# Attention with a gated feed-forward on one core: the maxima's split moves to VectorE, the output projection's operands come in two stages, and the order is written anew

## The chip, the cores and the metric

The kernel runs on one core of a Trainium2 chip. The core has a matrix engine (TensorE, PE in the profile; PEld is its weight loads), VectorE (DVE), ScalarE (ACT), GpSimd (POOL), and SyncE (SP), which here issues every transfer between the chip's memory (DRAM) and the on-chip buffers (SBUF). PE writes into PSUM, which has eight banks of 128 x 512 float32. The metric is the device time of one execution in microseconds. Lower is better.

## The reference

`x` is 2048 tokens of 512 numbers. There are 32 heads of 16 numbers and 1792 hidden units.

```python
xn  = layernorm(x)
q, k, v = heads_of(xn @ wqkv)                    # 32 heads, 16 wide
p   = softmax(q @ k.T * 16 ** -0.5)              # 2048 x 2048 for each head, no mask
s   = join(p @ v) @ wo
g   = silu(((xn @ w_gate) * (xn @ w_up)) @ w_down)
out = x + s * g
```

## The kernel before

**Numbers.** Most products are made of two roundings of each operand, "high" (the number cast to fp32r) and "low" (what the cast left out): three matmuls, high x high, high x low, low x high. So every operand of a projection has to be split first: a cast and a subtraction, on POOL for weights (`split_raw`, L247 and L250), hidden values (`hidden`, L435) and attention outputs (`o_split`, L763 and L764).

**Units.** Attention is cut into 32 units: 8 groups of four heads times 4 chunks of 512 queries. For a unit, `score` (L918) multiplies queries and keys into a PSUM bank, and VectorE reduces each bank to a maximum for each query over 512 keys (L920). When 64 of those are there, `maxima` (L926 to L929) takes the maximum over the four key chunks, negated, and splits it; `rest` (L936) transposes it on VectorE, stores it to DRAM (`MD`) and loads it back as two more rows of the unit's queries. `expo` (L946) then multiplies keys by queries with these rows, so that ScalarE's exponential (L948) is already shifted by the maximum. `pv` (L957) multiplies the exponentials with the values; a column of ones beside the values gives the sum. `heads` transposes (L984), divides (L971, L972), transposes back (L976) and stores the unit's heads to DRAM (`OD`).

**Outputs.** Beside the units run 218 "outputs": the projections, the feed-forward's gate, up and down products, and at the end the output projection. An output is a list of matmuls of 64 rows each (L465), done twice: once on the lower 64 rows of PE's array and later on the upper 64. Matmuls on the two halves run at the same time, as do the scores and exponentials of a unit's even and odd heads. `pv` uses all rows.

**The order.** PE, ScalarE and VectorE work in an order that is written by hand into a string, `ORDER`. Its letters: `f` and `F` the next matmul of an output on the lower and upper half, `o` a new output, `s`/`S` a score and its reduce, `t`/`T` a product for exponentials and the exponential, `v`, `w`, `z` one, two or three turns of `pv` (four heads each), `m` the maxima, `r` the rest of them, `x`, `c`, `b` the three steps of `heads`, `d` and `e` the evacuation of an output by VectorE or ScalarE, `l` a glance of ScalarE at a finished lower half (L495), `h` a hidden split, `y` the gate's silu, `Q` and a digit a call of `prepare`. A digit behind `s`, `t` or `o` names the PSUM bank that it takes. Instructions of POOL and the transfers of SP are put in order by the language's own scheduler after the mark `|` in the string (before it, POOL follows the string too); each engine and queue then works strictly in its order. So an instruction that waits holds up everything behind it on its engine.

**The feed-forward's end.** When a chunk's feed-forward is done, `silu` computes the gate for four tiles of 128 tokens in `y`; for the first three chunks each tile goes to DRAM (`YD`, L443) and is fetched again for the end.

**The end.** `prepare(c)` calls `o_split`, which loads chunk c's heads in four quarters of 128 numbers from `OD` and splits each on POOL. The first quarter goes through the raw buffer `w1r`, the second through `w0r`, the third and fourth through `wdr`, and each of these has one copy. The fourth quarter of chunk c holds groups 6 and 7, so it follows unit 28 + c; chunk 3's has only group 6, and group 7 is added by `final`. `z_out` then multiplies chunk c with `wo`, `end` (L787, L788) multiplies with the gate and adds `x`, and the result is stored. Chunk 3 is opened before (`open_out`) and closed after the last unit.

Of the kernel before, what the change touches and what calls it, by code (L numbers as in the profile page):

```python
# [44 lines left out]
0fFfFs3S4lzes5T1o0S3fT2fT4fFs1FfT5fFs3Ft2Fs4Ft1FfS5fFt2FfS3t4FfFfFs5S1efT2t3S4lwt6S5t2T3o1S4fFfFfS6fT5fFs4Ft2Fs3FfT6fF
fS5fT2s4Fmt3FfFs6FfFs5S2let4T3zo0T4rfS6fT3s5Ft2FfFs4Ft6Fs3FfT5fFfS2t6Fs4FfFt5FfS3fT6fFfS2s4S5elws3T6t1T2s4Fo5FfFt6Fs3F
fFs4FfT1fT2fFs3Ft6FfS4fT1fFfS2fFfS3et6T4lwxs2T1t0Fs3Ft6Fs4Ft1Fo2FfS0fFs3T6fFt4FfFfS1fT6fS0t3T4fFfFfS1fS6s3S0elzcs1T4s6
Fo5T3fFt0FfS4t1Ft3Fs6FfFt0Fs4FfT1fFfS6fT3s0FfFfS4efT1s6T3wfS0s4S6lt2T1o3FfFfFt0Ft2FfS4fFt1FfS6t0FfFfS4fT2t1Fs6FfS0fFt2
T4webfS6o1S0lt2T4fFfFfS5t6Fs2FfT0fS4fFs5T6fFt2FfFs0FfT6s4FfFfFs5T2ls0S6zems4T2o5T3fS0fT6fFfS2t4FfFt3S0fFt6S2fT4fFt0S3f
Fs6Ft2FfFfS4t3Fls0Ft6Fwers4T2s0Ft3Fs6Ft1Ft2Fo4FfFs0FfT3s1FfT6s2FfFfT3fS0fT1fFfS6fS2efS3t0T1lzt5S6s2T0t1Fo3FfFfS5t6FfS0  # L50
fT2fFs1Fs5T6fFfT0fFfS2t6Fs1FfFfFs5S0let6T2vxt4S1t6Fs5Fs0T2wcs1T4t6S5t2Fo0FfFs4FfT1fFs5FfT6s2FfT4fS1fFfT6fS5t2T4fFfFs1S
6lwet2S5t4Fs1Fo3Ft6FfS2fT5fFs1S4fT6fFt2FfS5fT1s6FfFt2Fs4FfFfS5efT1s6T2lzbs4T0s5Ft1Fs6Ft2Ft0Fo4FfFfS5fT1s2FfT6fS0fFfT1f
S5t2FfFfS6t1T0fFs5S2lwes6T1s5Ft0T3o2FfFfS1fFfT6s5Ft0FfS3t1FfS6fFt5FfS0mt3FfFfFs6S1efS5t0T3lzrt4S6o0Fs1T3t5FfFs4Ft6FfFf
S1fT3fS5t4Fs6FfFfT3fS1fT5fFfFs6Fls4S3et5T1wt2S6s4Ft5Fo1T3fFfS2fT6fS5t4FfFfS3t2Fs6Ft5FfFs4Ft2FfFfS3fS6efT5s4T2lwxt0S3t5
T2s6Fo4FfFfS0fFt3Fs5FfT6s2FfFfT3s0FfT5fS6fT2fFs3Fs0FfS5es6S2lzcs3T1s0Ft5T6o2FfFs1FfT3s5FfFfT0s6Ft1FfT3fS5fFfS0t6FfS1fF
s5T3fFt6T0lwes1T3t6S5t0Fo4FfFs3FfT1fS6fT5fFfS0t3Ft1Fs6FfFfS5t3FfS0fFfFs6S1let3S5zbs0T2t3S6t1Fo5FfFfS2t0Fs3FfFt6Fs1FfT2
t0FfS3fFmfFt6FfT2dfT1s3T0vt6S4s3T2fS1fT0whlrs4Ft6Fs3Ft2Ft0Fs1Ft6Fs4Fo3FfT2fS0fT1fFfS4fT6fS2fT0fFfS1s4FfS6et2T0lzt5S1o4
Ft2S6fFt0Fs5Ft1FfFfS6fT2fS0fT5fFs1FfT2fS6t0FfFfFs1Flt5T2s6Fs0Fwdxt5S1t2T6s0Fo3FfFfS5fT1fFfS2fT0s6Ft5FfFs1Ft0S2fFhfFfT5
fS6s1T0lwect5S2t0Fs6Fo1T4fFfS5fT2s0FfFt6Fs4Ft5Fs2FfT0s6FfFfT4fS5fFfS2fS0s6T4lzdho5T4s2T0t6FfS3fFfFfS4fT2fS0t3T6fFfFs4F
# [1061 lines left out]
```

## Time and profile before

| | |
|---|---|
| three runs | 1736.26, 1739.68, 1740.42 us; median 1739.68 |
| the profiled execution | 1738.24 us, its span 1736.5 us |
| mean granted clock of TensorE | 0.994 |
| busy: PE, DVE, ACT, POOL | 1710.6, 1427.1, 1222.9, 594.1 us |
| transfers | 145.81 MB, mean 84 GB/s |

The span is the time from the first to the last instruction. Lines such as L936 are lines of the kernel before. A row of a group has the line, the engine, the operation, the tiles written and read, the shapes and the count, then the busy time, the mean duration in ns and the idle time of the engine ahead of it. A row of a timeline has its start, its length, the engine and line, and, in brackets, how long the engine had been idle and what released it. A row of a waits view has who waited for whom, the total, how many times, and the longest.

### The profile page before, as it was taken

How to read it: one execution, taken by the hardware profiler on the slowest of the kernel's cores; microseconds unless marked ns; L12 is line 12 of the kernel's file. 1: busy time of each engine (PE TensorE's matmuls, PEld its weight loads, DVE VectorE, ACT ScalarE, POOL GpSimd, SP SyncE). 2: the span in 40 equal slices, each digit the busy share in tenths (PEclk: the TensorE clock that was granted, in tenths of full speed). 3: DMA queues.
4: the chain of work that ended last, by engine and by line, in shares of the span. 5: the costliest groups of instructions: out<-in, count | busy, mean ns of one | idle time of the engine just before them, and what ended most of it. 6: DMA issues, size and time to landing. Idle time of an engine off the chain costs nothing.

```text
span 1736.5 us, 35407 instructions
## 1 busy us (share of the span) xinstructions
PE 1710.6 (99%) x13792; PEld 1088.4 (63%) x13792; DVE 1427.1 (82%) x2401; ACT 1222.9 (70%) x2503; POOL 594.1 (34%) x681
## 2 busy tenths in 40 slices
...
DMA packets 119795, 145.81 MB, mean 84 GB/s; under 512 B 12620, under 2 KB 74060, under 8 KB 116940
## 3 DMA queue, kind: packets, MB, share of 16 engines
...
## 4 chain that ended last, share of the span: by engine, by line
PE 93%; DMA 2%; POOL 2%; issue 1%; DVE 1%; ACT 0%; POOLq 0%; SPq 0%; DVEq 0%
PE b L465 36%; PE pv L957 26%; PE b L946 15%; PE b L918 15%; DMA w0r<-in_wu_dram 1%; PE v L354 1%; DMA wdr<-OD 1%; POOL w0l L250 0%; DVE mx L920 0%; ACT e L948 0%; PE p L354 0%; DMA hh<-in_x_dram 0%; POOL dl L643 0%; DMA ks<-in_x_dram 0%; DMA w0r<-OD 0%
## 5 line engine op out<-in xcount | busy, mean ns | idle before, releaser
L920 DVE TENSOR_REDUCE mx<-b 128x1 f32<-128x512 f32 x2048 | 1277.4, 682 | 211.2 <-PE b L918 115.3
L948 ACT ACTIVATE e<-b 128x512 f32<-128x512 f32 x2048 | 1088.0, 601 | 375.8 <-PE b L946 230.3
L918 PE MATMUL b<-ks,qs 48*128 48x512 f32 x2048 | 749.8, 413 | 4.3 <-DVE mx L920 4.2
L946 PE MATMUL b<-qs,ks 50*128 50x512 f32 x2048 | 709.5, 416 | 3.4 <-DVE mx L920 3.4
L957 PE MATMUL pv<-e,V 128*32 128x512 f32 x4096 | 489.5, 598 | 0.0
L918 PEld LDWEIGHTS b<-ks,qs 48*128 48x128 f32 x2048 | 356.6, 185 | 142.7 <-DVE mx L920 57.7
L946 PEld LDWEIGHTS b<-qs,ks 50*128 50x128 f32 x2048 | 338.2, 185 | 161.0 <-ACT e L948 47.8
L957 PEld LDWEIGHTS pv<-e,V 128*32 128x32 f32 x4096 | 108.6, 109 | 231.8 <-issue 223.4
L465 PE MATMUL b<-fh,w1h 64*128 64x512 f32 x504 | 200.6, 400 | 0.2 <-DVE mx L920 0.2
L465 PE MATMUL b<-fh,w1l 64*128 64x512 f32 x504 | 198.8, 396 | 0.0
L465 PE MATMUL b<-fl,w1h 64*128 64x512 f32 x504 | 198.8, 395 | 0.0
L465 PE MATMUL b<-fh,w0h 64*128 64x512 f32 x500 | 198.4, 399 | 0.2 <-DVE mx L920 0.2
L465 PE MATMUL b<-fh,w0l 64*128 64x512 f32 x500 | 196.8, 396 | 0.0
L465 PE MATMUL b<-fl,w0h 64*128 64x512 f32 x500 | 196.8, 394 | 0.0
L465 PE MATMUL b<-dh,hh 64*128 64x512 f32 x448 | 161.9, 397 | 0.0
L465 PE MATMUL b<-dh,hl 64*128 64x512 f32 x448 | 159.0, 396 | 0.0
L465 PE MATMUL b<-dl,hh 64*128 64x512 f32 x448 | 158.9, 393 | 0.0
L247 POOL CAST w1h<-w1r 128x512 fp32r<-128x512 f32 x60 | 36.6, 611 | 270.3 <-DMA w1r<-in_wg_dram 97.4
L247 POOL CAST w0h<-w0r 128x512 fp32r<-128x512 f32 x60 | 36.6, 610 | 211.3 <-DMA w0r<-in_wu_dram 107.3
L465 PEld LDWEIGHTS b<-fh,w1h 64*128 64x128 f32 x504 | 93.9, 187 | 11.3 <-issue 3.5
L465 PEld LDWEIGHTS b<-fh,w0h 64*128 64x128 f32 x500 | 92.8, 186 | 8.5 <-issue 2.7
L465 PEld LDWEIGHTS b<-fh,w0l 64*128 64x128 f32 x500 | 92.7, 186 | 8.4 <-issue 3.4
...
## 6 DMA issues: line engine op xcount, KB each, us to landing
...
```

Source lines behind the costliest of these rows:

```text
L247: cast = nc.gpsimd.tensor_copy(hi, raw)
L354: nc.tensor.matmul(o, l(d), r(d), start=k == d == 0, stop=k == 2 and d == ND - 1)
L465: nc.tensor.matmul(self.o, l[rows], r[rows], start=x == 0 and n == 0, stop=last and (x == 0 or self.engine is not None), skip_group_check= ...
L918: nc.tensor.matmul(o, QS[i][b:b + KB, pr, t * P:(t + 1) * P], k[b:b + KB, pr, kc * 512:(kc + 1) * 512], start=True, stop=True)
L920: nc.vector.tensor_reduce(MX[i][:, j, t, kc:kc + 1], o, axis=AX.X, op=OP.max)
L946: nc.tensor.matmul(o, k[b:b + KR, pr, kt * P:(kt + 1) * P], QS[i][b:b + KR, pr], start=True, stop=True)
L948: fst["recent"] = fst["exp"] = nc.scalar.activation(e, o, AF.Exp, scale=DH ** -0.5).ins.name
L957: nc.tensor.matmul(fst["pv"][32 * j:32 * j + 32], V[:, kt, h0:h0 + 32], es[j], start=kt == 0, stop=kt == NT - 1)
```

## The change

Four things change.

1. In `maxima`, the high part of the negated maximum is no longer a cast on POOL of VectorE's result. VectorE does the reduce a second time, with the rounded type as its output, and VectorE does the subtraction.
2. `prepare` takes 0 to 6. For chunks 0, 1 and 2 the first call prepares the first three quarters; 4, 5 and 6 prepare the fourth quarter of chunks 0, 1 and 2. Chunk 3 is prepared at once, as before.
3. `silu` no longer queues the store of a gated tile at once. It is kept back and queued when the fourth output after it begins.
4. `ORDER` is another string from shortly behind the mark `|` to the end. The numbers of each kind of work are the same. In the new string `Q0`, `Q4`, `Q1`, `Q5`, `Q3`, `Q2`, `Q6` follow each other; before they were `Q0`, `Q3`, `Q1`, `Q2`. `Q4` and `Q5` stand shortly behind the `b` of units 28 and 29, and `Q2` and `Q6` stand together behind that of unit 30.

```diff
-FfFfFfFfFfFs2FfFs5Flo3FfS1efS6fFfFfFfFs2FfFfFs5Fs1FfFfFfFo0S6lefS2fFfFfFs5FfFfFs1Fs6FfFfFfS2fFfF|o4S5lefS1fFfFs6FfFfFf
...
+FfFfFfFfFfFs2FfFs5Flo3FfS1efS6fFfFfFfFs2FfFfFs5Fs1FfFfFfFo0S6lefS2fFfFfFs5FfFfFs1Fs6FfFfFfS2fFfF|o4S5lefS1fFfFs6FfFfFs
...
         nc.gpsimd.tensor_tensor(y[:, t], e, y[:, t], op=OP.mult)
         if c < NC - 1:
-            dma(YD[c][:, t], y[:, t])
+            order_.kept_back.append([4, lambda: dma(YD[c][:, t], y[:, t])])
...
+            self.kept_back = []
...
         def low_product(self, k=None):
             if self.low is None:
                 self.low = next(self.outs)
+                for w in self.kept_back:
+                    w[0] -= 1
+                while self.kept_back and self.kept_back[0][0] <= 0:
+                    self.kept_back.pop(0)[1]()
                 self.low.open(pool(k))
...
-    def o_split(c, tiles):
-
-        for d, (oh, ol) in enumerate(tiles):
+    def o_split(c, ds):
+
+        for d in ds:
+            oh, ol = ops[c][d]
...
-        ops[c] = tiles
...
-    def prepare(c):
-        if c in (0, 3):
-            o_split(c, small_tiles())
+    def prepare(n):
+        if n > NC - 1:
+            o_split(n - NC, [ND - 1])
+            return
+        if n in (0, NC - 1):
+            ops[n] = small_tiles()
         else:
-            if c == 2:
+            if n == 2:
                 last_weights()
-            h, l = fst["big", c]
-            o_split(c, [(h[:, d], l[:, d]) for d in range(ND)])
+            h, l = fst["big", n]
+            ops[n] = [(h[:, d], l[:, d]) for d in range(ND)]
+        o_split(n, range(ND if n == NC - 1 else ND - 1))
...
         mm = keep.tile([P, 4, 2, 4], F32R, name="mm", bufs=2)
-        nc.gpsimd.tensor_copy(mm[:, :, 0], m)
-        nc.gpsimd.tensor_tensor(mm[:, :, 1], m, mm[:, :, 0], op=OP.subtract)
+        nc.vector.tensor_reduce(mm[:, :, 0], MX[i], axis=AX.X, op=OP.max, negate=True)
+        nc.vector.tensor_tensor(mm[:, :, 1], m, mm[:, :, 0], op=OP.subtract)
```

More of the change, by code (lines that the diff above doesn't have):

```diff
@@ L45 @@
[L45 to L59, printed above, removed]
@@ L160 @@
[L160 to L162 removed]
+FfFfFfFfFfFs2FfFs5Flo3FfS1efS6fFfFfFfFs2FfFfFs5Fs1FfFfFfFo0S6lefS2fFfFfFs5FfFfFs1Fs6FfFfFfS2fFfF|o4S5lefS1fFfFs6FfFfFs
+2FfFfS5fFmfFfFfFs1Flo3S6efFfFs2FfFfFfFfFfS5fFfFfFrfS1o0FlfFs6FefFs2FfFfFs5FfFfFfS1fFfS6fFfFo4S2lfFs5FefFfFfFs1FfFfFs6F
+fFfFfS2fS5fFo3FlfS1efFfT6s2Ft5T0fFfFfS1fS6t2Fs5FfFfT0fS1fFo2FlfT6s0FfT5fFs1FfFes6Ft0T5fFfFs1Ft4Fs6Ft0FfFfS5t1FfS4fFs6F
@@ new lines @@
+fS0et1T5lzs4T3s6Ft1Fo0FfT5s3FfT4fS1t6FfFfS5s3FfT4fFt6Fs1FfT5s4FfT3fS6fFt5S1lwet3S4s6T5t2Fo1FfFs3Ft4Fs5FfFt6S2fFfT3fS4f
+T5fS6fFt2S3fFfFfFs4S5let2S6zo3T0s4FfT2fS5t6FfFs0Ft4FfS2t5FfFfT6s0FfFfS4fT5fT2s6FfFs0Flt5T4wemrt2S6s0Ft5Fo4FfT1fS2t6FfF
+s0Fs5T1fFt2FfS6fFt1FfS0fT5fFfFfS6es2S1lt0S5wt3S6s2Ft0Fo1FfT5s3FfT6fFs2T0fFfT5fS3fT6fFs2T0fFt5Fs3FfFs6Fs2S0ewfT5o3S6lfT
+4fS2fT0s5FfFt6Fs4Ft2Ft0FfFfT6s5FfFs4FfT2fFfT0s5FfS6s4S2elwxt0Fs5Ft1Ft6Fo4S2fT0fFfS5fT1fS6fT2fFfS0t5Fs1Ft6FfFfFs0Fs2S5e
+fS1zlct6T3s0Ft2Fo5S1fFfT6fFfS0t3Ft1FfS2fFs6FfT0t3FfFfS2fT1fS6s0Fls3Fwes2T1t4T6s0Fo3FfFfS1fFfT2s0T4fFfS6t1FfT2fFt0S4fFs
@@ new lines @@
+6FfFfFs1Fls4T2t0Ft6Fwebt2S1t0Ft6Fs4Fo5FfT2fS1fFfT0fS4t6FfFt2S1fFt0FfS4fFmfS6es1S2zrfT0o4S6lfT3fS1fT2fFs0Ft6Ft3Fs1FfFt2
+Fs0Ft6FfFs1T3fT2fFfS0fFt6T1fT3wels0T2o6T1fS3fFt5Fs2FfFfT0s3FfT1fS5t2FfFs0Ft3Fs1Ft5S2fFfFfS0efS3s1S5lzs2T4s0Ft3Fo1FfT5f
+S4t2FfS3t0FfFs5Ft4FfT2s3FfFfS0fT4s5FfFfS3efS2t4T0lvxt6T4t0Fs5Ft3T2wct6S5t4S0t3Fo2FfFfS6fT5fS4fT0s3FfFfT6s5FfT4fFfFs3Ff
+Fs5S0les6T4zs3T1o5T4t0S6fFfFfS1fT3s4FfT6fFt0Fs1FfFt3S4t6FfFs0FfT1fT3s4Ft6FwebfS0o1S4lfT3fFt6FfS2t0FfFs4Ft3FfS6t2Fs0FfF
+t3S4fFfT6fFfFfS0es2T3lt4S6ws0T5s2Fo3T4fT6fFfS5fT0fS4mfFt2T6fFfS5s0Ft4FfFs2Ft6FfFfFs5Fls0S4et6Fzrt1S2s5Ft6Fo0T4fFfS1t2F
@@ new lines @@
+s6FfFfT5fS4fT1s2FfT6fT5fFs4FfFfT1wls2Fs4Fet6T5o1FfFfS3t2FfS6t4FfFfS5t3FfS2t6Fs4FfFfT3fFfFfS5es2T6ls4T3wxt0Fs5Ft6Fs2Ft3
+Fs4Fo0Ft5FfS6t2FfFfS3fT5fS4fT6fFfFfS3efS2fS5t6T4lwct1S3s2T6t4Fo5FfFs1FfT3fS6fT2fFs4FfT1s3Ft6FfFfS2t1Fs4FfFfS3efS6s2S1l
+zt0S4t3S6o2T1fFfFs0Ft4Fs3FfT6fFs1FfT0fT4s3FfFfS6fT0fT1fFt4Flbs3Ft0S6wet1S3t4Ft0Fo6S5fFfS1fT3fFfT4s5FfT0fT1s3FfFs4Ft5Fs
+0FfFs3T1fFt5S4zdhmrfT1o0S3lfT5fS4fT2fFs1Ft3Ft5Fs4Ft2FfFs1FfFfT3fS4t5FfS2fFt3FfS1t4S5lwet3S2s1Ft4Fo5T6fFs3Ft2FfFfS1s4T6
+fFfT3fS2fFfT6s1FfT4s3FfFfFs2S6lt4T1zdht4S3t1Fs2Fo6FfT0fS4fT3fS1fT2fS0fFfT4s3Ft1FfFfS2t4Fs0FfFs3Flt1Fs2T4vexs0T1s3Ft4Ft
@@ new lines @@
+5S2wct1S0s3T4t5Fo2FfFfS1fT0fS4fT3fS5fFt1FfS0fT4fFs3Ft1Fs5FfFs0T4lwdhs3T1s5T4t0Fo6FfFfS1fT3fS4t5FfFs0FfT1s3Ft4FfFs5Ft1T
+0fFfS4fS3fFs5T1lzebt0S4t1T2o3S5fFfFfS0fT4fS1fT5fFs2FfT0s4Ft1FfFs5Ft0Fs2FfFt1T4fFs5S0lwds2T1t4T5s0Fo6FfFfS1fFfT2s0Ft4Ff
+S5t1FfFfS2t0FfS4hmt5FfFs1FfS2fT0welrt5S4s1Ft0T3o2FfFfS5fT4s0FfT1fFs3Ft5Fs4Ft0FfS1fFfT5fFfS3s4FfS0s1T5lzdht5S3s4Ft0Fo1F
+fT6fS5t3FfT0fS4fFfT6fS5t3FfFt0S4fFs6FfT5s3FfFt0Flt4s6S5wexs3T0t4Fs6T2o5FfFs0Ft3FfFt4Fs6FfT2fS0fT3fFs4FfT6fS2fT0fS3fFfS
+4fFfS6s2S0lzcds3T4t6Fs2Fs0Ft1Fs4Ft3Ft6Fo2FfFt1FfS0fT3fT4fS6fFs1FfT0fT3fFfS6fT4fS1fFfFs0S3let6S4ws1T5t6Fs0Ft3Ft4Ft5Fs1F
@@ new lines @@
+t6Ft0Fwbs1T3o4T5s6FfFfT0fS3fT1fFfS6fT5fS0fT3fFs1Ft5FfS6fFfS0efT3s1S5lwmt2S6t3Fs0T1o5FfFs2FfT6s3FfT0fS1fFt2FfS6t3Ft0FfF
+s1T2rfFfFs6FfFfFfS1efS3fS0s6S2lzt4S1t3Ft0S6o2FfFfS4fT1s3Ft6FfFfS0fT4t1Fs3FfT6fFt4S0fFfFs3T1fFs6Fls0Ft4Fhs3T1zes6T4s0Ft
+1Ft5Ft3Fs4Fs6Ft1Fo0FfT5fT4fS3fFfS6fFt1Fs5FfT3fS4fT6vext1T3t6S5t2T4wcfS5fT1o3S6lfS2fT4fT5s1FfFt6Fs4FfFt5Fs2Ft6T1fFfFfS4
+fFfS2fFs5S6ls1Ft4Fzdhs2T4t5Fs6Fs1Ft0Ft4Fo2FfS5fT6fT0fFfS1t4FfT5s6FfFfT0fFbfS1fT4s6S5lwes1T0s6Ft4Fs5Ft3Ft0Ft1Fo4FfS6fFf
+S3fT5fS0fFfT1fS6fT5fFs3FfFs0S1lt5T6wds3T5t6T0s1Fo2FfFfS5fT3fFt6S1fS0mfFt5Ft3FfFfS1t6FhfS0t5FfFfFs1S3lwers0T6t5Fs1Ft4Ft
@@ new lines @@
+3Fs6Fo0FfS5fT1fFfS4fT6fT3fS5fFfS1t6Fs4FfFs5S3fFs1S6lzds4T5s3T1o6T2fFfFfS5fT4fFt1S3fFfT2fS5t4FfFs3T1fFt2Fhs5FfFt4Flt1Fw
+ext2T4s3Fs5T1o0FfFfS2fFt3Fs4FfT5t1FfFs2FfT3fS4fT5fFfS1fFt3Fls2S4zcdhs1T5s2T3o4T6fFfFs5FfFt1Fs2T3fFfS6fT5s1FfFt2Ft3FfS6
+fFfFfS1et5S2lt3S6wt0S1t5T3o2S6fFfFfS0fT1fS5fT6fFfT3s0FfFt1S5fT6fFs3Ft0FfS1fFfFs5Fls3Fs6Fs0T1zbdt1S5t3Fo6S0fT4fFs1Ft5Fs
+3Ft0Ft4FfFfS1fT5fS3fT0fFfS4fT1t5FfS3fFs0Ft1FfFfS4s3T5lzdmrs0T1t5Fs4T3o2FfFfS1fT0fT5fS4fFfT3fS1t0FfFs4T5fFt3FfS1t0FfFs4
+Ft5Fs3Fs1FfS0fFt4S5lzds3T4t1T0o5S6fFfFs4FfT3t1Fs6FfFfS0t4Ft3FfFt1S6fFs0T4fFfFfS3fT6t1FfS0fFfFs3T4lwdxs0T6s3T1s2T4vs0T6
@@ new lines @@
+t1Fs3Ft4Fs2Ft6Fs0Fo1FfFfT3fS4t2FfFfS0t6FfS3t4T2fFcfFs0FfFhs3S6fS4fS2zlds0T3t6S4t2Fo5FfFs3FfT0fFfS4fT6t2Fs3FfT0fFfS4fT6
+fS2fFs3Flt0Ft4Ft6Fs2Fwet0S3o4T6t1S2fFfFfS0fT3s6FfFt2FfS1s0T3fFfT6fT2fFfS1t3Fls0Fs6Fbzdhs1T2s0T3t6Fo5FfFs2FfT1s3FfFfT0f
+S6t2Fs1Ft3FfFfS0t6S2fFfT1fFmfS3t6S0lwert1S2t6T4o3S0fFfFs1Ft2FfS6t0FfFfS4fT1t2FfS6fT0fFs4FfT1fFs6S2ls0Fs4Fzdt1S6t2S0t4F
+o5FfFfS1fT6fFs0T2fFfT4s1FfFfT6s0T2hfFs4FfFt6Fs1Ft0T2wext6T0s4S1s2T3vfT6o4S1lfT0fS3fT2s6FfFt1S0fFt3Fs2FfFt1Fs6Ft0FfFs3F
+fFct1S2t6T0vds3S1t6T2vhs5S3s1T0t6T2vs5S0s3T6vt2S1fS5fT6fo0S3lfT2fT1fFfS6t5FfFs3Ft2Fs1Ft6FfS5fFs3T2fFt1T6fFfFs5S2fFt1S3
@@ new lines @@
+lzdbt6Fo5S2t1FfS3t4FfFfS6fT2s1Ft3FfFs4FfT2fS6t1T3fFfFfS4fFs2Fls6S1t3Ft4Fwdms2T3s6Fo4T1fFt0Fs3Ft2FfFfS6fT1fS0fT3fFfS2t1
+S6fFt0FfFrfS3s2T1lwds6T0t1Fs3Ft2Fs5Fo0FfT6fFfS3fT1fS2fT5s6FfFt1S3fFfT2fFs5FfFs6S1ls3T2zds5T2t6T1s3Fo4FfFfS2t5FfFfS3fT6
+fS1fT2fS5fFt6Fs3Ft1Ft2FfFt6S5fFs3T1lvyxt2S5t6Fs3S1wecs5T2s3Ft6Ft0Fs1Fo2FfT5fS6fT3fFfT0fS1fT5fS6fFfT3fS0t1Fls5Ft6Fs3Fwy
+dht1S0s5Ft6Ft3Fs4Fo1FfT0fFfS5fT6s3FfT4fS0fFt6T5fFfS3fFfFs0Fls4S6es5Ft3Fzbs0T2o4T3s6FfT5fFs2FfT0fS3fFt6Ft5Fs2FfFt0S3fFf
+T6fFt5T2dfS0fS3wylhs1T6s0Ft5Ft2Fs3Ft6Fo1FfFfS0fT5s2FfT3fFfS6t5Fs0FfT2fS3mfFfS6efS5t0S2lzyrt4Fs3S6t0Fo5T2fFt4FfFfS3t0Fs
@@ new lines @@
+6FfT2fFfS4fT3s0FfT6fFt2FfS4fFt3S0lwdhs4T6t2S0t3Fo1FfFs6FfS4fT2fT0fFfS3fT6fS2fT4fFs0Ft3Fs6FfFs2Fls4Ft3T0wexo6T3fS2fT0fS
+4fT5fS3fFfT2s0Ft4FfFs5Ft2Fs3FfFt4Fs0Ft2T5fFfFs3S4lzcdht2S0o5T3fS4fT1fFfS2fFfT0fS4t3Fs1Ft2FfFs0Ft4FfS3t1FfFfFs0Fls2S4et
+1T3ws0T6t1T3s2Fo4FfFs6FfT0s1FfT2fFs3Ft6S0fFfT1fFs2Ft6S3fFfT0fFfS1s2T6lzbdhs3T0o1Ft6S2t5FfFs0FfFfT3fS2t6Fs5Ft0FfS3fFt2S
+6fFfT5fFfFfS3et0T2ls6S5wms3T4t0Fs6Fo2T5fFfS4fT3s0FfT6s5FfFt4FfS3t0FfFrs6Ft4T5fFfS3fFfS0fS4fS6fT5zldt5S3t0Ft4S6o1FfFfS5
+fT3fFs6T0fFfT4fS5fFt3FfS6fT0s4FfFt3S5fFt6Fs0FfFfFs4Flt3T5s6Fzexs0T3t5S4o6T2fFfFfS3fT0fFfS5t4S2fFt3FfFs0FfT4s5Ft2FfFs3F
@@ new lines @@
+fT4fS0t2T5fFfFs3S4lFt2S0czes3T5s4Ft2T1o0FfFfS5fT3s2FfT4fFs1Ft5Fs3Ft2FfFfS4t5T1fFfS2fFs3Ft5T4fFfS1fFfS2s3T5lzes1T4t5Fs2
+Ft6Fo3FfS4t1Fs5FfT2fFfS6t4Fs1FfT5fFs2Ft4T6fFfFs1FfS5fT4fFhbs2S6lwet4S1t0Fs5Fs2Ft6Fo4FfT1fS0t5FfS6fFfT2t1FfS0fFfT5s6FfF
+mfFfS0es2T1ls5T6zrs0T3s2T1t6Fo5FfFfS3fT0fFfS2t1Ft6FfS3fFt0FfS2fFfT1s3FfFs6Flt0T2s1Fwdht0S3t2T6o1S4fFfFfS0fT3fFfS4t2FfS
+6t0Fs3FfFt2Fs4FfT6fFs0FfS3et2ls4T6zxs0T5t2T6s3Fo4FfFs5FfFfT0fS2t3S6fFt5Fs0FfFs2T3fFfT6fFfS5fFs0T3lt6S2wcdt3S5s0Ft6Fs2F
+o1Ft3FfT5fFfS0t6FfS3fT2fFs5FfT0fS6t3FhfFfS2fFs5S0ls6T3zes2T3s5T4o0T6fFfFfS3t2Fs4FfFt5FfS6t3FfT2fS4t5FfFt6S3fFfFfFbt2S4
@@ new lines @@
+lwdht5S3t6S4t2Fo1FfFfS5fT3fFfS4fT6s2Ft5Fs3FfFfT6s4FfT2fFs5FfFs3T6ls4T2wes5T6t2T0o3S4fFfFfS6fT5fS2fT4fFms0Ft6FfS5t2FfFs
+4Ft6FfFfFs0Fls5S2t6Fzrdht6S4t0Fs5Fo2FfT1fS6t4Fs0FfT5fFfT1fS6fFs0T4fFfT5fS1t6FfFs0Flt4S5wet6S1t4Fs0Ft3Fs5Fo6FfT1fS4fT0f
+S3fFfT5fS1fT4fFs0FfT5fS3t1T4fFfFs0FfFs5S1lwdxt4Fs3Ft0Ft5Fs1Ft4Fs2Fs3S0wct5S1t4T2o3S0fFfFfS5fT1fFs0T4fFfT2s5FfT1fFs0FfT
+4fT2fS5fFfT1s0S4lwdt2S5t1Fs0Fs4Ft6Ft2Fs5Fo1FfT0fFfT6fS4fFt2S5fFt0FfS6t4FfS2fT5fFfS0fS6fFfS4s2Flzbdt5S0t6Ft4Fs2Fo3FfT5f
+S0fFfT6fS2fT4fFs0T5fFfT6s2Ft4FfFs0T5fFt6Fs2FfFfS4fFs0S5lzdmrs2T6s4Ft0Fs5Ft1Ft6Fo2FfFt0S4fFt1Fs5FfT6fFs4T0fFs1FfT5fFt6F
```

170 lines of the change are left out of this document (64 added, 106 removed).

## The prediction

> **What bounds the kernel now.** I read the page first, then the busy time by stretches, then the waits, then single stretches in order of time. The page says that TensorE (PE) is never long without work:
>
> ```profile
> span 1736.5 us, 35407 instructions
> PE 1710.6 (99%) x13792; PEld 1088.4 (63%) x13792; DVE 1427.1 (82%) x2401; ACT 1222.9 (70%) x2503; POOL 594.1 (34%) x681
> ```
>
> So the time is what PE's instructions take one after another, plus its stops. VectorE (DVE) is idle for 309 us, POOL for 1142 us; neither is a bound by its sum. The stretches show where PE stops (columns: length, then busy us of PE, PEld, DVE, ACT, POOL, then PE's granted clock, the DMA share and GB/s):
>
> ```profile
> 33.00:342.00 309.00, 309.00 (x2593) 217.17 (x2588) 254.42 (x425) 203.34 (x427) 122.24 (x141) 1.00 0.45 142
> 342.00:351.00 9.00, 7.50 (x52) 5.39 (x52) 5.38 (x10) 4.85 (x9) 2.52 (x6) 0.81 0.13 35
> 351.00:1102.00 751.00, 747.72 (x6126) 465.40 (x6120) 646.48 (x1075) 550.26 (x1129) 250.28 (x285) 1.00 0.23 63
> 1102.00:1110.00 8.00, 7.73 (x48) 6.21 (x52) 6.84 (x12) 5.15 (x10) 2.33 (x3) 0.79 0.14 38
> 1110.00:1643.00 533.00, 530.05 (x4291) 325.08 (x4283) 464.23 (x776) 391.06 (x792) 182.40 (x206) 1.00 0.25 69
> 1643.00:1662.00 19.00, 12.41 (x59) 9.01 (x62) 5.29 (x9) 6.27 (x13) 4.17 (x6) 0.64 0.26 81
> ```
>
> From 33 to 1643 us PE idles only 0 + 1.5 + 3.3 + 0.3 + 2.9 = 8.0 us. Between 1643 and 1662 alone it idles 6.6. Three of these stretches have a lower clock: 9 x 0.19 = 1.7 us, 8 x 0.21 = 1.7 us and 19 x 0.36 = 6.8 us of full clock are missing there. The waits say who ended the idle time (total, times, longest):
>
> ```profile
> DVE mt L936 <- POOL mm L929: 16.2, 5, 4.2
> PE b L465 <- POOL hl L763: 6.3, 2, 4.0
> PE b L918 <- DVE mx L920: 4.2, 2, 2.2
> PE b L946 <- DVE mx L920: 3.4, 3, 1.5
> DVE h L683 <- POOL hl L435: 2.0, 1, 2.0
> SPq L177 <- POOL y L441: 84.1, 12, 9.4
> ```
>
> 7.6 of the 8.0 us are five stops until a DVE maximum frees a PSUM bank (4.2 + 3.4), and DVE has five waits of its own, on POOL's half of the maxima. One of them, on POOL and then on PE:
>
> ```profile
> 340.28 0.61 POOL L247 CAST w0h<-w0r 128x512 fp32r<-128x512 f32 x1 [4.25 <-PE b L946]
> 342.74 0.20 POOL L928 CAST mm<-m 128x16 fp32r<-128x16 f32 x1
> 342.90 1.28 POOL L643 TENSOR_TENSOR dl<-wdr,dh 128x512 fp32r<-128x512 f32 x1
> 344.14 0.22 POOL L929 TENSOR_TENSOR mm<-m,mm 128x16 fp32r<-128x16 f32 x1
> ```
>
> ```profile
> 345.23 0.50 PE L946 MATMUL b<-qs,ks 50*128 50x512 f32 x1 [1.50 <-DVE mx L920]
> 346.26 0.62 PE L465 MATMUL b<-fh,w1h 64*128 64x512 f32 x1
> 346.69 0.62 PE L465 MATMUL b<-fl,w1h 64*128 64x512 f32 x1
> ```
>
> POOL was held by a weight split, so the two 0.2 us instructions of the maxima ended at 344.36; DVE's in-order transpose (L936) waited, the reduces behind it too, and PE had no bank. Just after the stop matmuls of one half come every 0.43 us.
>
> **The change part by part.**
>
> *The written order.* I counted both orders. The sums differ in two ways: runs of `v`, `w`, `z` (output products, "pv") that stand together are 241 before and 236 after; and where between two such runs the busier half of PE's rows decides, its slots add up to 4794 before and 4787 after. The number of products of every kind is the same. Prices from PE's timeline:
>
> ```profile
> 1096.07 1.92 PE L957 MATMUL pv<-e,V 128*32 128x512 f32 x16
> 1097.92 0.49 PE L946 MATMUL b<-qs,ks 50*128 50x512 f32 x1
> 1098.49 0.39 PE L946 MATMUL b<-qs,ks 50*128 50x512 f32 x1
> 1098.81 1.06 PE L957 MATMUL pv<-e,V 128*32 128x512 f32 x8
> 1102.08 0.50 PE L918 MATMUL b<-ks,qs 48*128 48x512 f32 x1 [2.20 <-DVE mx L920]
> 1636.98 1.06 PE L957 MATMUL pv<-e,V 128*32 128x512 f32 x8
> 1637.97 0.73 PE L918 MATMUL b<-ks,qs 48*128 48x512 f32 x3
> ```
>
> Two turns take 1097.92 - 1096.07 = 1.85 us, one takes 0.99, so a turn costs 0.86 and entering a run 0.13. The three slots from 1097.92 to 1098.81 take 0.89 where 3 x 0.23 would do: leaving and entering costs 0.2 more. A run's fixed price is about 0.33. 5 x 0.33 + 7 x 0.23 = 3.3 us less. If the halves are worse balanced at the seams than these rows show, it is 0.5 a run, so 3 to 4.
>
> *Maxima on VectorE.* Removed: 32 casts and 32 subtractions on POOL, and with them every wait of L936 on another engine. That is worth the 7.6 us of PE idle, if nothing else holds DVE up, and the clock lost right after two of the stops, 1.7 + 1.7: together 11.0. Bounds: 0 (the lateness moves, below) to 11.0; I take 11.0, because the five PE stops and the five DVE waits come in the same places and 0.4 us of idle is left for all else in 1610 us.
>
> [...]
>
> Added: a second reduce of 128x16 from 128x64 and a subtraction on DVE, per unit. Nearest rows:
>
> ```profile
> L926 DVE TENSOR_REDUCE m<-mx 128x16 f32<-128x64 f32 x32 | 6.7, 209 | 0.1
> L929 POOL TENSOR_TENSOR mm<-m,mm 128x16 fp32r<-128x16 f32 x32 | 7.1, 221 | 2.3
> ```
>
> 0.21 + 0.22 = 0.43 us a unit, 13.8 us in all, laid into DVE's 309 idle us. Cover gone, PE would wait 0.43 us each time, 13.8. The row it is nearest to is L926 itself: the like 0.21 us instruction at the same point of every unit leaves no stop in PE's idle time now. I take 1 us; bounds 0 and 13.8.
>
> *Operands in two stages.* The chain of waits before the stop at 1644:
>
> ```profile
> 1640.91 5.55 DMA wdr<-OD
> 1647.21 1.28 POOL dh L764
> 1648.51 4.12 DMA wdr<-OD
> 1653.37 1.28 POOL dh L764
> 1654.69 0.79 PE b L465
> ```
>
> Chunk 1's third and fourth quarters went one after the other through the single `wdr` buffer, both only after the heads of unit 29 were finished. PE idled 6.3 us for them (two stops, above). In the half clock from 1646.5 to 1660.2 some 4.7 us were idle anyway, so of the 6.8 us lost in that stretch 4.5 count: 10.8 with the stops. After the change the first three quarters are asked for about 28 us earlier by the order (82 slots, 9 turns and 5 runs before unit 29's `b`), with data long there; only the fourth has to follow unit 29. What it needs is shown by unit 28 now, which found queue and buffer free (DVE, SP and POOL in order of time):
>
> ```profile
> 1585.11 0.70 DVE L976 STREAM_TRANSPOSE tr<-on 128x512 f32<-128x512 f32 x1
> 1585.84 0.34 SPq L177 DMA_DIRECT2D OD<-tr  x1
> 1587.94 0.60 SPq L177 DMA_DIRECT2D wdr<-OD  x1
> 1592.01 0.61 POOL L763 CAST w0h<-wdr 128x512 fp32r<-128x512 f32 x1 [9.23 <-DMA wdr<-OD]
> 1592.69 1.29 POOL L764 TENSOR_TENSOR w0l<-wdr,w0h 128x512 fp32r<-128x512 f32 x1
> ```
>
> 7.5 us to the high half. In the new order 25 slots, 4 turns and 3 runs lie between unit 29's `b` and the first product of the fourth quarter: 5.8 + 3.4 + 1.0 = 10.2 us. `c` now stands directly ahead of `b`, and DVE may be a microsecond or two behind. That leaves 0 to 2 us. SP waits 2.1 us with this load for the store to land; chunk 3's loads and those of the gated values queue behind it and are needed tens of us later. I take 1.5 us of stop; bounds 0 and 10.8. For chunk 2 both stages stand in one place, which changes nothing; the 16 loads remain 16.
>
> *Gated stores.* SP's 84.1 us of waiting for `y` go, as each store is queued only when the fourth output after its gate starts. Those waits delay weight loads and POOL's splits; where that reached PE it is in the 11.0 already, or in the one 2.0 us wait of DVE on L435. What hides the stores' later place: the `y` buffer is written again at the thirteenth output of the next chunk, in the new order at least two outputs after the last store is queued, 16 us at 1736.5 / 218 us an output. With that cover gone ScalarE's copy into `y` would be late, and the exponentials behind it. I take 0; bounds -2.0 and 0.
>
> **Sum.** 1736.5 - 3.3 - 11.0 + 1 - 10.8 + 1.5 = 1713.9 us of span. The profiled execution took 1738.24, and the median of the three runs is 1739.68, 3.2 above the span. 1713.9 + 3.2 = 1717.1.
>
> **The rivals.**
>
> *The fourth quarter stays late* (A). The new order gives it 10.2 us where the old gave 31 slots, 7 turns and 6 runs, 15.1 us, and there it failed. For it: half-clock stretches make any short stop dear. Against: the failure came from loads queued ahead in one buffer. Price: between half and all of the 10.8 returns, 1722 to 1727.
>
> [...]
>
> *The change moves POOL's lateness and doesn't remove it* (C). POOL's weight splits still wait for PE and loads, and the hidden split (L435) is in the same queue; DVE's L683 waits for it, as once now. The new order could place it where POOL is late. Price: the 11.0 return, and with some of A's 10.8, 1728 to 1739. Against it: one such wait in 56.
>
> *DVE becomes the bound at each maximum* (D), the slower side. Banks are filled again after some five slots, 1.2 us, and a reduce takes 0.68. If 0.43 us more at every maximum stops PE, and each stop brings a low-clock stretch of 1.7 us, one unit costs 2.1 us. From 11 of 32 units on the 22.6 us gained are gone; with 16, 1751. For it: DVE is 82% busy. Against: the transpose of 0.2 us behind every maximum does no harm now.
>
> **Chances.** Forecast 0.52, A 0.17, B 0.08, C 0.14, D 0.09. The forecast's own range goes from 1712 (1717.1 less the 2.5 us of taken costs, less the 2.0 on L435, with 0.7 for the run) to 1723 (half of the 10.8). The range for 8 in 10 takes in A, B and most of C: 1709 to 1735. A measurement of this kernel tells 0.3%, 5.2 us, from no change. Faster than 1734.5: forecast, A, B and two thirds of C, 0.86, less 0.05 for an order whose stops are unseen, 0.81. Within: the rest of C and a little of D, 0.11. Slower: 0.08.
>
> **What would show it.** No wait of L936 on POOL; PE's idle from 33 us to the start of the last outputs under 2 us and its clock 1.00 there; pv entries of 1.85 and 0.99 us as now; the casts of chunk 1's first three quarters before unit 29's transpose, and PE's wait on L763 under 2 us. It is wrong if waits on DVE's reduces grow after the maxima, if PE waits for L763 by over 4 us, or if low-clock stretches come without a stop ahead of them.

## The result, and the profile after

The changed kernel takes 1711.8 us (four runs, 1711.33 to 1712.08) against 1738.71 us for the kernel before (four runs, 1736.26 to 1740.42). The ratio is 0.9846, with a 95% interval from 0.9829 to 0.9863: faster by 1.5%. The forecast was 1717.1, with a range from 1709 to 1735.

The page of the changed kernel, and its busy time by stretches (columns as before):

```profile
span 1708.6 us, 35418 instructions
PE 1695.8 (99%) x13792; PEld 1089.4 (64%) x13792; DVE 1440.7 (84%) x2464; ACT 1221.5 (71%) x2503; POOL 583.7 (34%) x618
```

```profile
33.00:342.00 309.00, 308.90 (x2589) 219.06 (x2587) 256.70 (x438) 203.18 (x426) 121.10 (x131) 1.00 0.45 142
351.00:1102.00 751.00, 750.97 (x6158) 472.75 (x6158) 659.25 (x1117) 555.97 (x1137) 242.45 (x253) 1.00 0.23 63
1110.00:1620.00 510.00, 509.53 (x4160) 317.04 (x4156) 451.17 (x765) 374.34 (x763) 174.67 (x183) 1.00 0.25 69
```

```profile
33.00:1640.00 1607.00, 1606.40 (x13202) 1033.82 (x13198) 1397.32 (x2368) 1161.68 (x2383) 553.57 (x580) 1.00 0.28 81
```

From 33 to 1640 us PE's idle time is 0.6 us (the last row, 1607.00 less 1606.40), where 8.0 + 6.6 were lost before, and the clock is 1.00 throughout. So of the 27.9 us between the two spans 14.0 are stops that are gone, and 7.9 are the clock that was lost after them (1.7 + 1.7 + 4.5, as in the prediction). That leaves 6.0 for the written order and for what the rows do not show.

Among the waits neither the transpose on POOL nor PE on an operand split appears. These two rows do; the first is the longest wait of PE's matmuls from 33 to 1640 us:

```profile
PE b L465 <- ACT look L500: 0.4, 1, 0.4
SPq L177 <- POOL y L441: 83.6, 12, 8.8
```

The second row is the surprise. SP waits for the gated tiles as it did before, 83.6 us in 12 times against 84.1 in 12.

The groups of the maxima, all on VectorE now (busy us, mean ns, idle before):

```profile
L938 DVE TENSOR_TENSOR mm<-m,mm 128x16 fp32r<-128x16 f32 x32 | 8.8, 276 | 1.1
L935 DVE TENSOR_REDUCE m<-mx 128x16 f32<-128x64 f32 x32 | 6.7, 210 | 0.1
L937 DVE TENSOR_REDUCE mm<-mx 128x16 fp32r<-128x64 f32 x32 | 6.7, 209 | 0.0
L945 DVE STREAM_TRANSPOSE mt<-mm 128x32 f32<-128x32 f32 x32 | 6.5, 203 | 0.2
```

The subtraction's mean is 276 ns, not the 221 of POOL's. The transpose (L945) has 0.2 us of idle ahead of it, where 16.2 us of waiting for POOL stood before.

### The profile page after: what moved, and what is told of

Read it like the earlier page. It is cut to its first block, busy times and chain, and to the rows that moved or that the text cites. A ratio compares the mean times of both kernels' runs of the same rounds, so it can differ in the third digit from the quotient of the medians.

```text
span 1708.6 us, 35418 instructions
## 1 busy us (share of the span) xinstructions
PE 1695.8 (99%) x13792; PEld 1089.4 (64%) x13792; DVE 1440.7 (84%) x2464; ACT 1221.5 (71%) x2503; POOL 583.7 (34%) x618
## 4 chain that ended last, share of the span: by engine, by line
PE 97%; DVE 1%; POOL 1%; issue 0%; DMA 0%; ACT 0%; POOLq 0%; SPq 0%; DVEq 0%
PE b L465 37%; PE pv L966 27%; PE b L955 16%; PE b L927 15%; PE v L354 1%; PE p L354 0%; DVE mx L929 0%; DMA ks<-in_x_dram 0%; POOL dh L770 0%; PE b L332 0%; POOL y L441 0%; PE xT L317 0%; POOL hl L769 0%; ACT ks L295 0%; POOLq L1122 0%
## 5 line engine op out<-in xcount | busy, mean ns | idle before, releaser
L955 PE MATMUL b<-qs,ks 50*128 50x512 f32 x2048 | 722.4, 414 | 0.2
L955 PEld LDWEIGHTS b<-qs,ks 50*128 50x128 f32 x2048 | 342.4, 184 | 159.4 <-issue 48.6
L465 PEld LDWEIGHTS b<-fh,w1l 64*128 64x128 f32 x504 | 93.1, 185 | 8.8 <-issue 3.4
L465 PEld LDWEIGHTS b<-fl,w1h 64*128 64x128 f32 x504 | 93.3, 186 | 5.1 <-issue 0.8
```

Source lines behind the costliest of these rows:

```text
L465: nc.tensor.matmul(self.o, l[rows], r[rows], start=x == 0 and n == 0, stop=last and (x == 0 or self.engine is not None), skip_group_check= ...
L955: nc.tensor.matmul(o, k[b:b + KR, pr, kt * P:(kt + 1) * P], QS[i][b:b + KR, pr], start=True, stop=True)
```

## The experiments

All of them were timed beside the kernel before on the same chip, whose median in those comparisons was 1737.2 to 1737.8 us. Two medians of the same kernel before can so differ by 1.5 us (1738.71 above, 1737.24 here); a difference of that size between two runs below shows nothing.

### The two removals, each alone, in the old order

Maxima on VectorE only, in the kernel before:

```diff
-        nc.gpsimd.tensor_copy(mm[:, :, 0], m)
-        nc.gpsimd.tensor_tensor(mm[:, :, 1], m, mm[:, :, 0], op=OP.subtract)
+        nc.vector.tensor_reduce(mm[:, :, 0], MX[i], axis=AX.X, op=OP.max, negate=True)
+        nc.vector.tensor_tensor(mm[:, :, 1], m, mm[:, :, 0], op=OP.subtract)
```

> The kernel before, its old order kept, with only the maxima's cast and subtraction moved to VectorE. My theory: the five stops on VectorE's maxima and the two low-clock stretches after them go, 11.0 us, and the stop at 1643 stays with its low clock: 1727 to 1729, ratio about 0.994. Rival (the new order is what removed the stops; in the old one POOL's lateness only shows elsewhere): 1735 to 1739, with VectorE waiting for POOL's hidden split or PE for weights instead. Rival (two more VectorE instructions a unit cost time where banks are tight): above 1732, with more PE idle on VectorE's reduces.

Measured: 1726.26 us, ratio 0.9935 [0.992, 0.995], 11.5 us less, a little below the expected 1727 to 1729. The five stops and both short low-clock stretches are gone; the mean granted clock is 0.996, 0.994 before. The stop on chunk 1's operands is still there:

```profile
PE b L465 <- POOL hl L763: 5.9, 2, 4.0
```

Two stages only, in the kernel before, with the letters

```diff
-... Q0 ... Q3 ... b Q1 ... Q2
+... Q0Q4 ... Q1 o(second output of the projection) ... Q3 ... b Q5 ... Q2Q6
```

> The kernel before with only the two-stage preparation: the fourth quarter of chunk 0 right behind its first three, the first three of chunk 1 asked for ahead of the second output of the output projection, its fourth where all four were, chunk 2 as before; all else of the old order kept. My theory: the two stops of PE on L763 (6.3 us) and the 13.65 us low-clock stretch go, 10.8 us, and the five stops on the maxima stay: 1727 to 1730. Rival (the fourth quarter alone is late too, about 15 us of PE time after unit 29 in the old order): half of it stays, 1733 to 1739. Rival (the low clock does not come from the stops): the stops go but the low clock at about 1646 stays, 1732.

Measured: 1727.93 us, ratio 0.9942 [0.9927, 0.9958], 9.8 us less. The 13.65 us low-clock stretch went with the stop: the clock from 1640 to 1725 us is 1.00. In this string `Q1` also stands ahead of `Q3`, where it stood behind it before; that matters further down. The waits show that the other cause is untouched (line numbers have moved by four, L940 is the transpose):

```profile
DVE mt L940 <- POOL mm L933: 16.3, 5, 4.3
PE b L465 <- POOL dh L765: 0.6, 1, 0.6
PE b L465 <- POOL hl L764: 0.5, 1, 0.5
```

Both edits in the old order:

> Both of the two edits above in the old order. My theory: they add up, 1738.7 - 21.8 = 1717 to 1719, and what is left to the changed kernel's 1711.8 is the order: 3 to 6 us. Rival (the order did more than its five runs and seven slots): 1722 or more.

Measured: 1718.16 us, ratio 0.9889 [0.9872, 0.9905], 19.6 us less. 11.5 + 9.8 = 21.3 would be the plain sum, so they add up but for 1.7 us, which the spread of the runs (1717.0 to 1719.1) does not settle. From here to the changed kernel's 1711.8 are 6.4 us, and they are put down to the order (with the stores, which the next experiment takes out).

### The stores

The changed kernel with the gated tiles stored at once:

```diff
-            order_.kept_back.append([4, lambda: dma(YD[c][:, t], y[:, t])])
+            dma(YD[c][:, t], y[:, t])
```

> The changed kernel with the gated tiles' stores queued at once again. The changed kernel's trace shows SyncE waiting 83.6 us in 12 times for the gated tiles, as before the change (84.1 in 12), and each store issued 0.03 us after its tile is done. Theory: the language's scheduler puts the stores in the same place of SyncE's queue either way, so this edit does nothing here: 1711 to 1713, the same 12 waits. Rival: the stores now block weight loads: 1714 or more, with more POOL waits for loads around 610, 940 and 1270 us.

Measured: 1711.49 us, ratio 0.9851 [0.9835, 0.9868], no difference to the changed kernel. SP's wait is the same to a tenth of a microsecond:

```profile
SPq L177 <- POOL y L441: 83.5, 12, 8.8
```

In the traces of the two runs SP issues the same 564 transfers in the same order. Moving the call later in the program did not move the store in the queue. So this run can't say what SP's waits for the tiles cost, since they are there with the edit and without it.

### The maxima in the new order

The changed kernel with the cast and the subtraction back on POOL:

> The changed kernel with the maxima's cast and subtraction back on POOL, in the new order. My theory: the new order has the same kind of weight splits on POOL ahead of the maxima, so some of 32 transposes wait for POOL again and PE stops after them: 1716 to 1725, with low-clock stretches after the longer stops. Rival (the new order by itself keeps POOL free at the maxima): 1712 and no wait of the transpose on POOL.

Measured: 1729.38 us, ratio 0.9955 [0.994, 0.997]: 17.6 us more than the changed kernel, and more than either theory had. The waits:

```profile
DVE mt L945 <- POOL mm L938: 29.9, 15, 4.6
PE b L955 <- DVE mx L929: 6.8, 5, 2.8
PE b L927 <- DVE mx L929: 3.0, 3, 1.3
PE b L465 <- DVE mx L929: 1.5, 1, 1.5
```

The transpose waits for POOL 15 times, not five. PE's stops are 6.8 + 3.0 + 1.5 = 11.3 us, and four low-clock stretches of 3.413 us cost 1.7 each, 6.8 (the mean granted clock of 0.996 leaves 6.9 of the span of 1730.2 us missing); the sum is 18.1. The new string has `r` close behind `m`: within about 6 us of PE time, and in seven units with nothing or almost nothing between, where the old string left 3 to 10. That fits an order that counts on POOL being out of the way.

### What VectorE's additions cost

The changed kernel with the second reduce done three times:

```diff
-        nc.vector.tensor_reduce(mm[:, :, 0], MX[i], axis=AX.X, op=OP.max, negate=True)
+        for _ in range(1 + 2):
+            nc.vector.tensor_reduce(mm[:, :, 0], MX[i], axis=AX.X, op=OP.max, negate=True)
```

> The changed kernel with the second reduce of the maxima done three times, which writes the same values: 0.25 to 0.42 us more of VectorE for each of 32 units. My theory: VectorE has room at the maxima: 1711 to 1713. Rival D (VectorE is at its limit there): 8 to 13 us more, and with a low-clock stretch for every stop up to 60: 1720 or more.

Measured: 1718.77 us, ratio 0.9891 [0.9876, 0.9906], 7.0 us more than the changed kernel and between the two expectations. One unit's maxima in its timeline, then PE's stretch from 33 to 1640 us:

```profile
236.35 0.21 DVE L935 TENSOR_REDUCE m<-mx 128x16 f32<-128x64 f32 x1
236.47 0.72 DVE L938 TENSOR_REDUCE mm<-mx 128x16 fp32r<-128x64 f32 x3
237.23 0.17 DVE L939 TENSOR_TENSOR mm<-m,mm 128x16 fp32r<-128x16 f32 x1
```

```profile
33.00:1640.00 1607.00, 1604.48 (x13146) 1028.89 (x13144) 1406.30 (x2423) 1157.40 (x2370) 551.04 (x578) 1.00 0.28 81
```

Three reduces into one tile take 0.72 us, 0.51 more than one, 16 us over 32 units. 7.0 of those 16 reach the end. So VectorE has little room at the maxima in the new order, though it is idle for 16% of the changed kernel's span. Little of the loss shows as idle time of PE: 2.5 us in this stretch against 0.6 in the changed kernel. But PE gets through 13146 matmuls there and not 13202, and at 1607 us / 13202 = 0.122 us a matmul the 56 missing ones are 6.8 us. So a late bank can cost PE time where PE is not idle, as its matmuls then come further apart. PE's clock did not fall in this stretch; the longest single stop is 0.8 us.

The other direction, with two of the three instructions taken out. The shift's low part stays zero; softmax divides any shift out, so the output is the reference's:

```diff
+    shift = [keep.tile([P, 4, 2, 4], F32R, name=f"mm{n}") for n in range(2)]
+    for mm in shift:
+        nc.gpsimd.memset(mm.bitcast(F32), 0.0)
...
-        m = keep.tile([P, 4, 4], F32, name="m", bufs=2)
-        nc.vector.tensor_reduce(m, MX[i], axis=AX.X, op=OP.max, negate=True)
-        mm = keep.tile([P, 4, 2, 4], F32R, name="mm", bufs=2)
+        mm = shift[i % 2]
         nc.vector.tensor_reduce(mm[:, :, 0], MX[i], axis=AX.X, op=OP.max, negate=True)
-        nc.vector.tensor_tensor(mm[:, :, 1], m, mm[:, :, 0], op=OP.subtract)
```

> The changed kernel with the shift's low part left at zero: softmax divides the shift out, so the rounded maximum alone serves. One reduce a unit is left of the three VectorE instructions. Two more reduces cost 7.0 us, 0.11 us each. If VectorE's time at the maxima is on PE's path in the same way below as above: 3 to 8 us less, 1704 to 1709. Rival (the order hides just these two, so that only what is added shows): 1710 to 1712.

Measured: 1709.66 us (1709.62 to 1711.04), ratio 0.9842 [0.9828, 0.9857]. That is at most 2 us less, and neither expectation: what is added costs 7.0, what is taken out gives 2 or nothing, as the intervals of the two kernels overlap. The new order hides most of the two instructions that it was written with.

### One stage or two, in the new order

The changed kernel with the old `prepare`, `Q0` and `Q1` at the places of `Q4` and `Q5`:

> The changed kernel with the operands prepared in one stage again, chunks 0 and 1 at the place of their fourth quarters in the new order (behind units 28 and 29), chunks 2 and 3 as they are. My theory: chunk 1's four quarters follow unit 29, two of them through the one wdr buffer, with only 10 us of PE time until the first is read; PE stops on the splits for 8 to 14 us and loses clock for 4 to 7 more: 1722 to 1732. Rival (the new order's places alone removed the stop): 1712 to 1714.

Measured: 1709.97 us (1709.66 to 1710.92), ratio 0.9842 [0.9827, 0.9856]. My theory fell: without the two stages nothing stops, and the time is no longer. Nor is it shown to be shorter: the spans of the two profiled executions are 1707.5 and 1708.6 us, and the lead of 1.1 us is there before the edit acts. This run, then the changed kernel in its first 33 us, then this run from 33 to 1640 us:

```profile
0.00:33.00 33.00, 29.07 (x148) 20.73 (x148) 25.16 (x72) 20.27 (x37) 17.95 (x26) 1.00 0.78 264
0.00:33.00 33.00, 27.46 (x140) 19.80 (x142) 26.23 (x70) 19.85 (x36) 17.93 (x26) 1.00 0.80 264
33.00:1640.00 1607.00, 1606.62 (x13202) 1033.86 (x13199) 1397.20 (x2366) 1162.49 (x2383) 553.60 (x580) 1.00 0.28 82
```

It is eight matmuls ahead after 33 us, 1.0 us at 0.122 us each, and from there to 1640 us it does the same 13202 as the changed kernel. Of chunk 1's first three quarters in its trace, the first and the third on POOL, and unit 29's transpose on VectorE:

```profile
1580.04 0.61 POOL L768 CAST hl<-w1r 128x512 fp32r<-128x512 f32 x1 [5.82 <-PE b L465]
1583.66 0.63 POOL L768 CAST hl<-wdr 128x512 fp32r<-128x512 f32 x1
```

```profile
1610.86 0.71 DVE L981 STREAM_TRANSPOSE tr<-on 128x512 f32<-128x512 f32 x1
```

The string asks for all four quarters behind unit 29, and three of them are split 27 to 31 us ahead of it. (The 13 us in an expectation below is a misreading of mine; the rows give 27.) So the scheduler moves loads ahead of their place in the string. My reading is that it can't change the sequence in which a single buffer is handed out, and in the old string chunk 3 stood ahead of chunk 1 for `wdr`. The trace of the kernel before fits it (SP, PE and POOL in order of time):

```profile
1594.01 0.58 SPq L177 DMA_DIRECT2D wdr<-OD  x1
1628.60 0.39 PE L465 MATMUL b<-fh,w0l 64*128 64x512 f32 x1
1629.76 0.61 SPq L177 DMA_DIRECT2D w1r<-OD  x1
1631.59 0.62 POOL L763 CAST w0h<-wdr 128x512 fp32r<-128x512 f32 x1
1636.42 0.45 SPq L177 DMA_DIRECT2D OD<-tr  x1
1639.62 1.27 POOL L764 TENSOR_TENSOR w0l<-wdr,w0h 64x512 fp32r<-64x512 f32 x1
```

Chunk 3's third quarter is loaded into `wdr` at 1594.01 and lies there until it is split at 1631.59. The split writes tiles that chunk 0's operands use too, and PE reads those until 1629.0. Chunk 3's fourth quarter follows, its split ends at 1640.89, and the load of chunk 1's third quarter is issued at 1640.91. That quarter needs nothing of unit 29 (it holds groups 4 and 5). Chunk 1's first quarter, in `w1r`, is loaded at 1629.76 even here, ahead of the store of unit 29's heads at 1636.42.

Two runs put the reading to the test. In the kernel before, one letter moved:

```diff
-... Q3 ... b Q1 ... Q2
+... b Q1Q3 ... Q2
```

> The kernel before with one letter moved: chunk 3's preparation stands behind chunk 1's instead of ahead of it. One stage, old order, maxima on POOL. The changed kernel with one stage ran no slower, and its trace shows chunk 1's first three quarters split about 13 us ahead of unit 29's last transpose, though the string asks for them behind it. New theory: the scheduler asks for loads early anyway, and what held chunk 1 up was chunk 3's two quarters standing ahead of it in the single wdr buffer; moving the letter alone gives what the two stages gave in the old order: 1727 to 1730, PE's wait on L763 under 1 us. Rival (the two stages are what does it in the old order): 1735 to 1739.

Measured: 1731.49 us, ratio 0.9962 [0.9948, 0.9977], 6.2 us less and not 9.8. PE no longer waits for L763 at all. But a new wait has come soon after:

```profile
1650.33 0.61 POOL L763 CAST w0h<-wdr 128x512 fp32r<-128x512 f32 x1 [4.09 <-DMA wdr<-OD]
1656.37 0.60 POOL L763 CAST w0h<-wdr 64x512 fp32r<-64x512 f32 x1 [4.07 <-DMA wdr<-OD]
1658.26 0.19 POOL L928 CAST mm<-m 128x16 fp32r<-128x16 f32 x1
1658.53 0.22 POOL L929 TENSOR_TENSOR mm<-m,mm 128x16 fp32r<-128x16 f32 x1
```

```profile
DVE mt L936 <- POOL mm L929: 5.9, 1, 5.9
```

Chunk 3's quarters come later now, POOL waits for their loads, and the last unit's maxima wait behind them on POOL. PE then stops for 2.8 us, and a stretch of 3.4 us at half clock follows at 1661.11, worth 1.7 more (the clock from 1640 to 1725 us is 0.98). So the letter removes the stop on the operands, and this second loss, through the first cause, accounts for the 3.6 us that are missing from the 9.8 as far as the runs' spread (1727.7 to 1732.8) can tell.

The reverse, in the changed kernel with one stage: chunk 3 ahead of chunk 1.

```diff
-... b Q1 ... Q3 ... Q2
+... b Q3Q1 ... Q2
```

> The changed kernel with one stage (the run that took 1709.97), and with chunk 3's preparation moved ahead of chunk 1's, as in the old order. New theory: the stop on chunk 1's splits comes back with its low clock, 8 to 14 us: 1718 to 1724. Rival (the new order leaves room whatever stands first): 1710 to 1712.

Measured: 1732.79 us, ratio 0.9968 [0.9958, 0.9979], 22.8 us more than with the letters the other way round, and well above what I expected. PE's stops in its timeline, then the stretch around them:

```profile
1625.49 0.50 PE L465 MATMUL b<-fh,hl 64*128 64x512 f32 x1 [3.14 <-POOL hl L768]
1626.86 0.79 PE L465 MATMUL b<-fh,dh 64*128 64x512 f32 x1 [0.63 <-POOL dh L769]
1636.21 0.79 PE L465 MATMUL b<-fh,hl 64*128 64x512 f32 x1 [8.56 <-POOL hl L768]
```

```profile
1621.00:1650.00 29.00, 12.68 (x72) 7.98 (x68) 7.92 (x13) 5.95 (x12) 9.42 (x10) 0.65 0.32 100
```

The stretch has 16.3 us of idle, 15.4 of it put down to the casts (L768), and a mean clock of 0.65. That the loss is larger than in the old order may be because the new one leaves only 10 us, by the prediction's estimate, between unit 29's end and the first use; no run separates that.

The high part alone together with one stage:

> The same in the changed kernel with one stage. If the one stage's 1.5 us are real and add up: 1 to 2 us below the run e12; if they were noise: as e12.

Measured: 1709.93 us (1709.21 to 1711.41), ratio 0.9843 [0.9828, 0.9858]. This is the time of the high part alone, the second case of the expectation. None of the three versions at 1709.7 to 1710.0 is told apart from the changed kernel by the intervals.

### A ladder of hold-ups

Added reduces in seven units alone, 8 to 40 of them:

> The changed kernel with the second reduce repeated 8, 12, 16, 20, 24, 32 and 40 times more in units 8, 11, 14, 17, 20, 23 and 26 alone: VectorE is held up there by about 1, 1.6, 2, 2.6, 3, 4 and 5 us (0.13 each) or by half as much again (0.2 each). It shows from which length on a hold-up of VectorE stops PE, and which stops lower the clock. My theory: the first 0.5 to 1 us are hidden, then PE stops nearly microsecond for microsecond, and stops from about 1.5 us on are followed by a low-clock stretch of 3.4 us now and then; 1722 to 1735. [...]

Measured: 1756.86 us in one run, over 20 us above the expected 1722 to 1735. An added reduce took 0.25 us, as in the run with three (0.51 for two), and not 0.13 to 0.2, so the seven hold-ups were 2.0 to 10.2 us long and not 1 to 5, or half as much again. PE's stops were 0.6 us after the first, 1.8 after the second, 3.5 after the third and 4.4 to 9.2 after the others, so 0 to 1.7 us of each hold-up were hidden. After the first two the clock stayed, after the other five it fell; the mean granted clock is 0.988, 21 us of full clock missing in a span of 1755.1. With stops of 3.5 us and more from the third on, this run does not show whether a shorter one is enough; the rows of the kernel before in the last section do.

## Why the prediction was right or wrong

**The maxima: right, size nearly so.** 11.0 less 1 for VectorE's additions, 10.0, was forecast; 11.5 was measured in the old order with the additions paid. The way was the forecast one: POOL late, transpose late, reduces late, a bank late, PE stopped, and then the clock. In the new order the move is worth 17.6, which the prediction could have seen, since it had both strings: the new one has `r` up to 6 us closer to `m`.

**VectorE's additions: 1 us forecast, 0 to 2 measured** (1711.8 less 1709.66, with intervals that overlap). The row it was taken from, a like instruction that stopped nothing, was the right one, but it stood for the old order. Rival D was nearer than its chance of 0.09 says: another 0.51 us of VectorE a unit cost 7.0 us. The low clock that the rival counted with did not follow.

**Operands in two stages: right time, wrong cause.** 10.8 was forecast and 9.8 measured in the old order. The step that failed is "only the fourth has to follow unit 29", taken as what the second stage brings. In the new order the stages bring nothing (1709.97 without them), as the scheduler fetches the first quarters ahead in any case. There the stop went because chunk 1 stands ahead of chunk 3 in the buffer's sequence; the other way round costs 22.8 us. That the time came out is luck: in the string that asks for the first three quarters earlier, chunk 1 also stands ahead of chunk 3. The prediction said that both of chunk 1's last quarters were late "only after the heads of unit 29 were finished"; the third waited for chunk 3's two quarters in `wdr`. The single buffer was in its chain of waits, and its rival A even speaks of "loads queued ahead in one buffer", but whose loads they were was not looked for. The 1.5 us put aside for a late fourth quarter were not needed in the new order: no wait of PE on it is left. In the old order 0.4 to 1.1 us of it are.

**The stores: right size, wrong step.** "SP's 84.1 us of waiting go" is false. 83.6 stay, the queue is the same with the edit and without it, and the effect is nothing because nothing moves. Whether those waits hold up anything that PE needs stays open.

**The order: 3.3 forecast, 6.4 measured.** This is the largest miss of the sum. What was left out is VectorE's wait for the hidden split (L435): it was 2.0 us before, is 2.2 in the run with both edits in the old order, and is gone in the changed kernel. The prediction bounded it at 2.0 and took 0. The run with both edits shows its price (VectorE's wait, then 60 us of that run and of the changed kernel):

```profile
1285.90 0.69 DVE L683 TENSOR_TENSOR h<-b,g 128x512 f32<-128x512 f32 x1 [2.16 <-POOL hl L435]
1280.00:1340.00 60.00, 59.70 (x479) 38.06 (x476) 50.47 (x87) 45.78 (x92) 32.01 (x34) 1.00 0.45 97
1280.00:1340.00 60.00, 60.00 (x496) 37.04 (x492) 53.40 (x92) 45.91 (x95) 30.04 (x31) 1.00 0.45 96
```

PE does 17 matmuls fewer in the run with both edits, 2.1 us at 0.122 each, with only 0.3 us of it idle. Counted in the same way, 20 matmuls (2.4 us) are gained between 1580 and 1640 us, and the rest lies spread over the units; what of that is the fewer runs of `pv` and the slots was not separated.

**The sum.** 1713.9 of span was forecast and 1708.6 measured. Of the 5.3 between them 3.1 are the order's. The two edits in the old order gave 19.6, where 19.3 was forecast (10.0 and 10.8 less 1.5). The remaining 1.9 lie within the spread of the runs of the kernel before.

**The rivals.** A (fourth quarter late) did not come. B (the low clock has other causes than PE's stops) is out: the three stretches, at 346, 1104 and 1646 us before, are gone with the stops, the first two in the run with the maxima alone and the third in the run with the stages alone. C (the lateness moves) did not come in the changed kernel, but the run with one letter moved shows that it can. D: above.
